# Expert layers of a mixture-of-experts kernel: the first layer's weights become the stationary operand, and the two layers swap which weights stay on chip

## The chip, the core and the metric

The kernel runs on one core of one Trainium2 chip. Its engines are named as in the profile: PE is TensorE's matmul stream and PEld its weight loads, DVE is VectorE, ACT is ScalarE, POOL is GpSimd, and SP is SyncE, which here only issues DMAs. The metric is the device time of one execution in microseconds (us). Everything is computed in float32.

## What is computed

Block-sparse attention over 4 batch entries, 8 heads, 768 tokens and a head size of 64 gives x, 3072 tokens of width 512. A router then sends each token to one of 8 experts, and each expert is two layers with a relu between them. The attention and the router are not changed; this is the part that is:

```python
N, D, E, F = (3072, 512, 8, 1024)
...
logits = x @ w_gate
expert_idx = np.argmax(logits, axis=1)
...
for e in range(E):
    lo, hi = (boundaries[e], boundaries[e + 1])
    if lo == hi:
        continue
    h = np.maximum(x_sorted[lo:hi] @ w1[e], 0.0)
    y_sorted[lo:hi] = h @ w2[e]
y = y_sorted[inv_perm]
return (gate_w[:, None] * y).astype(np.float32)
```

An expert's w1 is 512 x 1024 and its w2 is 1024 x 512, so either is 2 MB, and all eight of either are 16 MB.

## The kernel before

The kernel has three stages. The first is the attention, with the router's logits behind each pair of heads. In it x is written to a DRAM tensor `x_rows`, a token to a row of 520 numbers (512 of x, its gate weight, and room). At the very start POOL also issues the eight loads of all of w1 (`load_w1`, L94) into the resident tile `w1_all`, while SP loads the first heads' q, k and v.

The second stage (L297 to L411) sorts: from the logits DVE works out `xe`, the expert of each of 31 tiles of 128 tokens, and `g_idx` and `s_idx`, the rows that a tile gathers and scatters. The tokens of an expert start on a new tile, so at most 24 + 7 = 31 tiles are needed, and 31 are always run.

The third stage runs the 31 tiles. For tile i:

- `gather(i)` (L424, POOL, indirect DMA) brings 128 rows of x into `xg`, which has 4 buffers.
- `fetch(i)` (L430 to L432, SP) reads the tile's expert from `xe` into a register (a value load: TENSOR_LOAD and two register operations) and loads that expert's w2, 2 MB, into one of two buffers.
- `turn_x(i)` (L437) transposes the four 128 x 128 blocks of `xg` on PE into PSUM (`tpg`), and DVE copies them to `xgT` (L439).
- `layer1(i)` (L447) makes h, 128 tokens x 1024, in two PSUM banks: 8 matmuls, `xgT` as the stationary operand (the one that a weight load brings into the array) and 512 columns of `w1_all` as the moving one. A float32 matmul is two instruction pairs in the trace, each a weight load and a matmul, so this is 16 pairs. DVE does the relu of one half (L452) and ACT of the other (L453).
- `turn_h(i)` (L460) transposes h in eight blocks on PE, since the second layer needs it with its 1024 features on the partitions; DVE (L462) and ACT (L464) copy the result to `hT`.
- `layer2(i)` (L469) makes 128 tokens x 512 from 8 matmuls (16 pairs), `hT` stationary and 512 columns of the fetched w2 moving. DVE multiplies by the gate weight (`zo`, L471), and POOL scatters the rows to the output (L472).

In the source, tile i + 1's `turn_x` and `layer1` stand ahead of tile i's `turn_h` and `layer2`, and the fetch for tile i + 2 stands behind `layer2(i)`. The final order on each engine is not the source's: a scheduler of the framework orders the instructions from the dependencies and its own estimates. Each engine then runs its list in order, and a wait in a list holds up all that stands behind it there. The value loads of an engine are such list entries too.

Of the kernel before, what the change touches and what calls it, by code (L numbers as in the profile page):

```python
# [8 lines left out]
F32 = mybir.dt.float32  # L9
# [9 lines left out]
def kernel(  # L19
# [12 lines left out]
    P = 128  # L32
# [4 lines left out]
    NCH = S // P  # chunks of 128 tokens; chunk c holds the tokens NCH * p + c  # L37
    CW = NCH // 2 * P  # columns of half the chunks, within one PSUM bank
# [7 lines left out]
    NC = NT + E - 1  # tiles that the tokens take at most, each of one expert  # L46
    XW = DM + 8  # a token's row in DRAM: x, its gate weight, and room
    scale = 1.0 / float(D) ** 0.5
    # Added to a score before the scale; a masked one then lies near -1e9, whatever it was.
# [12 lines left out]
    w1_all = big.tile([P, DB, E, F], F32, name="w1_all")  # L62
# [30 lines left out]
    def load_w1(e):  # L93
        nc.gpsimd.dma_start(w1_all[:, :, e, :], moe_w1[e].rearrange("(c p) f -> p c f", p=P))  # L94
# [5 lines left out]
    def make_mask(pool):  # L100
        # Which blocks of keys (columns) a block of queries (partitions) attends to.
# [24 lines left out]
        # rows[n, t, p]: whether query NCH * p + t lies in block n.  # L126
# [38 lines left out]
    def scores(b, pr, t):  # L165
# [11 lines left out]
        for hh in range(2):  # L177
            # The scores with their sign turned, and the least of each row: minus its maximum.
# [41 lines left out]
    def route(b, pr, half, xb):  # L220
        # What the pair's columns of x add to the logits, for half of the chunks.
# [46 lines left out]
    for u in range(len(units) + LAG):  # L268
        if u < len(units):
# [7 lines left out]
            if t == 3 and n % 2 == 0 and n // 2 < E:  # L277
                load_w1(n // 2)
# [53 lines left out]
    # The first of the experts with the greatest logit.  # L332
# [9 lines left out]
    # Ranks within the expert, and how many tokens each has.  # L342
# [10 lines left out]
    # Tiles by expert, and the tiles up to and with each expert's.  # L353
# [8 lines left out]
    # The expert of each tile.  # L362
# [8 lines left out]
    # Each token's slot, from 0.  # L371
# [15 lines left out]
    # The token of each slot plus one, 0 for none.  # L387
# [31 lines left out]
    w2v = moe_w2.rearrange("e (a p) d -> p e a d", p=P)  # L419
# [9 lines left out]
    def fetch(i):  # L429
        e = nc.sync.value_load(xe[0:1, i : i + 1], min_val=0, max_val=E - 1)  # L430
# [50 lines left out]
    for i in range(2):  # L481
        gather(i)
        fetch(i)
    turn_x(0)
    layer1(0)
    for i in range(NC):
        if i + 2 < NC:
            gather(i + 2)
# [37 lines left out]
```

## Time and profile before

| | |
|---|---|
| time, median of 3 runs | 1203.21 us (1201.95 to 1203.82) |
| the profiled execution, span | 1203.9 us |
| attention, up to its last score tiles | 0 to 668.0 us |
| the sort, and the wait for the first gathers | 668.0 to 701.3 us |
| the 31 tiles, first layer-1 matmul to last layer-2 matmul | 701.3 to 1195.3 us |
| the last scatter | 1195.3 to 1203.9 us |

The profiled execution's span lies 0.7 us above the median of the timed runs. In the rows of the trace a line of a timeline is a run of equal instructions: its start, how long the run took, the engine, the source line, the operation, what it writes and reads, the shapes and the count; in brackets stands the idle time before it and what ended it. A row of PE or PEld covers latency too: the last of a run of matmuls is reported until its result is written, so the pace of a run is read from the starts, or from the run's length less the length of one. Buffers whose names differ by a number are written as one, so `w_all` is `w1_all` before and `w2_all` after, and `w` is a fetched weight tile.

### The profile page before, as it was taken

The page shows a single profiled execution, that of the slowest core. Times are in us where ns is not written, and L with a number is a line of the kernel's source. Part 1 is how long each engine was busy: PE and PEld are TensorE (multiplying, and loading weights), DVE is VectorE, ACT ScalarE, POOL GpSimd, SP SyncE. Part 2 cuts the span into 40 slices and gives each one's busy share as a digit, 9 for nine tenths or more (in the row PEclk, how much of TensorE's full clock was granted, in tenths as well). Part 3 has the DMA queues.
Part 4 walks back from the last instruction along what each step waited for, and adds up shares of the span by engine and source line. Part 5 has one row for each costly group of instructions (what it writes and reads, how often), then busy time and mean ns, then how long its engine had stood idle before and what let it go on. Part 6 is the DMA issues. An engine that isn't in the chain of part 4 may idle for free.

```text
span 1203.9 us, 15693 instructions
## 1 busy us (share of the span) xinstructions
PE 1131.7 (94%) x6132; PEld 756.1 (63%) x6132; DVE 414.1 (34%) x1032; ACT 355.5 (30%) x707; POOL 73.8 (6%) x101
## 2 busy tenths in 40 slices
PE   2899999999999999999999579999999999999996
PEld 1687878787877788788878534444444444444443
DVE  1654545554454444454444411111111111111110
ACT  0454545454545455455545000000000000000000
POOL 3000000000000000000000011111110111111100
PEclk9999999999999999999999679999999999999998
DMA  9911221112021212120000415544444555544441
GB/s 337 343 37 27 54 53 28 40 43 53 27 52 30 53 27 54 27 54 27 27 1 14 154 36 174 168 141 160 149 156 164 175 172 175 174 162 149 161 140 55
DMA packets 112269, 122.64 MB, mean 102 GB/s; under 512 B 56451, under 2 KB 72835, under 8 KB 112196
## 3 DMA queue, kind: packets, MB, share of 16 engines
q1 hardware_dynamic: 102484, 90.28, 24.9%
q0 software_dynamic: 9184, 31.33, 6.7%
q8 instruction: 50, 0.82, 0.3%
q14 instruction: 23, 0.19, 0.1%
q10 hardware_dynamic: 528, 0.02, 0.0%
HBM read 108.93 MB, written 14.52 MB: 103 GB/s over the span
## 4 chain that ended last, share of the span: by engine, by line
PE 54%; issue 38%; POOL 3%; DVE 2%; DMA 1%; SPq 0%; POOLq 0%; ACT 0%; DVEq 0%
PE op L209 21%; PE s L173 16%; PE tpe L197 12%; POOL xg L424 3%; PE lg L230 2%; PE tp L155 2%; DMA samp_i<-in_sampled_blocks_dram 1%; POOL out_dram L472 1%; PE tpx L225 1%; PE tok_ps L404 1%; DVE mask L142 0%; DVE wide L141 0%; PE bm L136 0%; SPq L84 0%; DVE oh_r L399 0%
## 5 line engine op out<-in xcount | busy, mean ns | idle before, releaser
L209 PE MATMUL op<-v_sb,eT 128*128 128x64 f32 x2304 | 278.5, 271 | 0.0
L209 PEld LDWEIGHTS op<-v_sb,eT 128*128 128x128 f32 x2304 | 272.4, 192 | 0.0
L186 ACT ACTIVATE e<-e,nmax 128x768 f32<-128x768 f32 x192 | 179.7, 936 | 243.6 <-DVE nmax L181 238.8
L447 PE MATMUL hp<-w_all,xgT 128*128 x496 | 223.2, 604 | 16.4 <-DVE xgT L439 16.4
L469 PE MATMUL zp<-w,hT 128*128 128x512 f32 x496 | 218.2, 593 | 1.1 <-DVE hT L462 1.1
L181 DVE CUSTOM_DVE_ANT_0 e<-s,mask 128x768 f32<-128x768 f32 x192 | 176.3, 954 | 103.2 <-PE s L173 103.2
L173 PE MATMUL s<-kT,qT 64*128 64x384 f32 x768 | 198.3, 525 | 7.8 <-DVE nmax L181 7.8
L447 PEld LDWEIGHTS hp<-w_all,xgT 128*128 128x128 f32 x496 | 92.7, 192 | 129.2 <-issue 105.9
L197 PEld LDWEIGHTS tpe<-ident,e 128*128 128x128 f32 x1152 | 127.5, 145 | 61.1 <-issue 26.7
L197 PE MATMUL tpe<-ident,e 128*128 128x128 f32 x1152 | 164.5, 279 | 0.0
L469 PEld LDWEIGHTS zp<-w,hT 128*128 128x128 f32 x496 | 91.8, 190 | 105.3 <-issue 103.8
L464 ACT COPY hT<-tph 128x512 f32<-128x512 f32 x31 | 18.2, 586 | 436.7 <-PE tph L460 436.7
L201 ACT COPY eT<-tpe 128x512 f32<-128x512 f32 x192 | 110.8, 577 | 51.0 <-PE tpe L197 50.5
L173 PEld LDWEIGHTS s<-kT,qT 64*128 64x128 f32 x768 | 79.2, 188 | 45.1 <-issue 19.6
L471 DVE TENSOR_SCALAR zo<-zp,xg 128x512 f32<-128x512 f32 x31 | 23.3, 750 | 204.3 <-PE zp L469 204.3
L452 DVE TENSOR_SCALAR h<-hp 128x512 f32<-128x512 f32 x31 | 21.4, 691 | 209.0 <-PE hp L447 209.0
L199 DVE COPY eT<-tpe 128x512 f32<-128x512 f32 x96 | 65.9, 687 | 15.5 <-PE tpe L197 15.3
L472 POOL DMA_INDIRECT out_dram<-zo,s_idx x31 | 31.6, 1018 | 431.3 <-DVE zo L471 431.3
L213 DVE TENSOR_SCALAR r<-ss 128x2 f32<-128x2 f32 x96 | 16.1, 167 | 88.1 <-ACT e L186 88.1
L215 DVE TENSOR_TENSOR xb<-op,r 128x128 f32<-128x128 f32 x96 | 28.0, 292 | 43.9 <-PE op L209 42.8
L308 POOL IOTA first_w_i<- 128x8 int32 x1 | 0.1, 135 | 657.4 <-PE op L209 657.4
L460 PEld LDWEIGHTS tph<-ident,h 128*128 128x128 f32 x248 | 30.0, 141 | 16.4 <-issue 16.4
(103 smaller groups left out, 484.0 us busy)
## 6 DMA issues: line engine op xcount, KB each, us to landing
w<-in_moe_w_dram SPq DMA_DIRECT2D x31, 2048.0 KB, 10.4
w_all<-in_moe_w_dram POOLq DMA_DIRECT2D x8, 2048.0 KB, 27.3
k_sb<-in_k_dram SPq DMA_DIRECT2D x32, 192.0 KB, 3.4
q_sb<-in_q_dram SPq DMA_DIRECT2D x32, 192.0 KB, 3.3
v_sb<-in_v_dram SPq DMA_DIRECT2D x16, 384.0 KB, 3.4
x_rows<-xb SPq DMA_DIRECT2D x16, 384.0 KB, 4.3
xg<-x_rows,g_idx POOLq DMA_INDIRECT x31, 7.8
out_dram<-zo,s_idx POOLq DMA_INDIRECT x31, 8.0
```

Source lines behind the costliest of these rows:

```text
L173: nc.tensor.matmul(sps[hh][:, j, :CW], lhsT=qT[r, t * P : (t + 1) * P], rhs=kT[r, j * CW : (j + 1) * CW], start=True, stop=True,)
L181: nc.vector.tensor_tensor_reduce(out=e.rearrange("p (j c) -> p j c", j=2), in0=sps[hh][:, :, :CW], in1=mask[:, t, :].rearrange("p (j c) -> ...
L186: nc.scalar.activation(e[:], e[:], AF.Exp, bias=nmax[:], scale=-1.0, accum_out=ss[:, hh : hh + 1])
L197: nc.tensor.transpose(tp[:, m, :], es[hh][:, c * P : (c + 1) * P], ident[:])
L199: nc.vector.tensor_copy(part[:], tp[:])
L201: nc.scalar.copy(part[:], tp[:])
L209: nc.tensor.matmul(op[:, hh, :], lhsT=eT[hh * NCH + c], rhs=v_sb[:, hh, c, :], start=(c == 0), stop=(c == NCH - 1),)
L424: nc.gpsimd.indirect_dma_start(out=xg[:], out_offset=None, in_=x_d[:, :], in_offset=bass.IndirectOffsetOnAxis(ap=g_idx[:, i : i + 1], axis=0),
L447: nc.tensor.matmul(hp[:, f, :], lhsT=st[i]["xT"][:, c, :], rhs=w1_all[:, c, bass.ds(e, 1), f * 512 : (f + 1) * 512].rearrange("p e f -> p ...
L460: nc.tensor.transpose(tp[:, m, :], st[i]["h"][:, (4 * g + m) * P : (4 * g + m + 1) * P], ident[:])
L469: nc.tensor.matmul(zp[:], lhsT=st[i]["hT"][:, fb, :], rhs=st[i]["w2"][:, fb, :], start=(fb == 0), stop=(fb == FB - 1))
L472: ins = nc.gpsimd.indirect_dma_start(out=out[:, :], out_offset=bass.IndirectOffsetOnAxis(ap=s_idx[:, i : i + 1], axis=0), in_=zo[:], in_of ...
```

## The change

All of w2 is now loaded at the start and stays resident (`w2_all`), and each tile's w1 is fetched instead. With w1 in a tile buffer, `layer1` takes 128 x 128 blocks of w1 as the stationary operand and the 128 tokens of `xgT` as the moving one, so that its result comes out as h with the features on the partitions. The relu writes `hT` directly; `turn_h`, the tile h and its two copies are gone. The value load on PE moves from `layer1` to `layer2`, and `fetch` moves ahead of `gather` for the first two tiles and from behind `layer2` to beside the gather for the others.

```diff
-    w1_all = big.tile([P, DB, E, F], F32, name="w1_all")
+    w2_all = big.tile([P, FB, E, DM], F32, name="w2_all")
...
-    def load_w1(e):
-        nc.gpsimd.dma_start(w1_all[:, :, e, :], moe_w1[e].rearrange("(c p) f -> p c f", p=P))
+    def load_w2(e):
+        nc.gpsimd.dma_start(w2_all[:, :, e, :], moe_w2[e].rearrange("(a p) d -> p a d", p=P))
...
         e = nc.sync.value_load(xe[0:1, i : i + 1], min_val=0, max_val=E - 1)
-        w2 = st[i]["w2"] = wp.tile([P, FB, DM], F32, name="w2")
-        nc.sync.dma_start(w2[:], w2v[:, bass.ds(e, 1)].rearrange("p e a d -> p (e a) d"))
+        w1 = st[i]["w1"] = wp.tile([P, DB, F], F32, name="w1")
+        nc.sync.dma_start(w1[:], w1v[:, bass.ds(e, 1)].rearrange("p e c f -> p (e c) f"))
...
     def layer1(i):
-        e = nc.tensor.value_load(xe[0:1, i : i + 1], min_val=0, max_val=E - 1)
-        hp = ps_h.tile([P, 2, 512], F32, name="hp")
-        h = st[i]["h"] = xp.tile([P, F], F32, name="h")
-        for f in range(2):
-            for c in range(DB):
-                nc.tensor.matmul(
-                    hp[:, f, :], lhsT=st[i]["xT"][:, c, :],
-                    rhs=w1_all[:, c, bass.ds(e, 1), f * 512 : (f + 1) * 512].rearrange("p e f -> p (e f)"),
-                    start=(c == 0), stop=(c == DB - 1),
-                )
-        nc.vector.tensor_relu(h[:, :512], hp[:, 0, :])
-        nc.scalar.activation(h[:, 512:], hp[:, 1, :], AF.Relu)
-
-    def turn_h(i):
+
         hT = st[i]["hT"] = xp.tile([P, FB, P], F32, name="hT")
         for g in range(2):
-            tp = ps_m.tile([P, 4, P], F32, name="tph", tag="m")
-            for m in range(4):
-                nc.tensor.transpose(tp[:, m, :], st[i]["h"][:, (4 * g + m) * P : (4 * g + m + 1) * P], ident[:])
+            hp = ps_h.tile([P, FB // 2, P], F32, name="hp")
+            for m in range(FB // 2):
+                fb = g * (FB // 2) + m
+                for c in range(DB):
+                    nc.tensor.matmul(
+                        hp[:, m, :], lhsT=st[i]["w1"][:, c, fb * P : (fb + 1) * P], rhs=st[i]["xT"][:, c, :],
+                        start=(c == 0), stop=(c == DB - 1),
+                    )
             if g == 0:
-                nc.vector.tensor_copy(hT[:, :4, :], tp[:])
+                nc.vector.tensor_relu(hT[:, : FB // 2, :], hp[:])
             else:
-                nc.scalar.copy(hT[:, 4:, :], tp[:])
+                nc.scalar.activation(hT[:, FB // 2 :, :], hp[:], AF.Relu)
 
     def layer2(i):
+        e = nc.tensor.value_load(xe[0:1, i : i + 1], min_val=0, max_val=E - 1)
...
     for i in range(2):
+        fetch(i)
         gather(i)
-        fetch(i)
     turn_x(0)
     layer1(0)
     for i in range(NC):
         if i + 2 < NC:
             gather(i + 2)
+            fetch(i + 2)
         if i + 1 < NC:
             turn_x(i + 1)
             layer1(i + 1)
-        turn_h(i)
         layer2(i)
-        if i + 2 < NC:
-            fetch(i + 2)
```

What the scheduler makes of it is seen in the order of instructions. First PE in the steady part of the third stage, before: one tile, from the end of one layer 2 on (the two value loads stand in the first tiles only).

```order
L469 MATMUL zp<-w2_6334,hT 128x512 x8
L437 MATMUL tpg<-ident,xg 128x128 x4
L460 MATMUL tph<-ident,h 128x128 x4
L442 TENSOR_LOAD xe
L442 ISA x2
...
L447 ISA
L447 MATMUL hp<-w_all,xgT 128x512
...
L460 MATMUL tph<-ident,h 128x128 x4
```

The same place after.

```order
L438 MATMUL tpg<-ident,xg 128x128 x4
L463 ISA
L463 MATMUL zp<-w_all,hT 128x512
L463 ISA
L463 MATMUL zp<-w_all,hT 128x512
L450 MATMUL hp<-xgT,w_6631 128x128 x32
L463 ISA
L463 MATMUL zp<-w_all,hT 128x512
```

Between the transposes of x and the first layer that reads them there stood four transposes of h; now two of the eight layer-2 matmuls of the tile before stand there, and the other six follow the first layer.

Second, PE at the start of the third stage, before: behind the last of 17 value loads two tiles' transposes and then the first layer.

```order
L442 TENSOR_LOAD xe
L442 ISA x2
L437 MATMUL tpg<-ident,xg 128x128 x8
L447 ISA
L447 MATMUL hp<-w_all,xgT 128x512
```

And after.

```order
L438 MATMUL tpg<-ident,xg 128x128 x16
L460 TENSOR_LOAD xe
L460 ISA x2
L460 TENSOR_LOAD xe
L460 ISA x2
...
L450 MATMUL hp<-xgT,w_6319 128x128 x32
```

Four tiles' transposes, and behind them five of the value loads, have moved ahead of the first tile's first layer.

Third, SP at the same place, before: the first fetch stands behind one value load.

```order
L255 DMA x_rows<-gw 768x1x8
L430 TENSOR_LOAD xe
L430 ISA x2
L432 ISA
L432 DMA w_6321<-in_moe_w2_dram 128x8x512
L430 TENSOR_LOAD xe
```

And after, the last of the value loads ahead of the first fetch, and the two fetches.

```order
L431 TENSOR_LOAD xe
L431 ISA x2
L433 ISA
L433 DMA w_6319<-in_moe_w_dram 128x4x1024
L433 ISA
L433 DMA w_6332<-in_moe_w_dram 128x4x1024
```

Seventeen value loads now stand ahead of the first fetch.

## Rows read from the trace of the kernel before

**Rows 1.** The page: span, then each engine's busy time, share and instructions.

```profile
span 1203.9 us, 15693 instructions
PE 1131.7 (94%) x6132; PEld 756.1 (63%) x6132; DVE 414.1 (34%) x1032; ACT 355.5 (30%) x707; POOL 73.8 (6%) x101
```

**Rows 2.** Sums by stretch: length, busy time per engine (instructions), granted clock, DMA share, GB/s.

```profile
0.00:60.00 60.00, 33.07 (x193) 24.59 (x194) 23.51 (x61) 15.96 (x31) 9.56 (x23) 1.00 0.99 340
701.30:1195.30 494.00, 476.47 (x1357) 226.99 (x1356) 80.45 (x122) 33.71 (x62) 56.94 (x57) 1.00 0.45 151
```

**Rows 3.** Timeline of PE over one tile of the third stage.

```profile
909.27 0.60 PE L460 MATMUL tph<-ident,h 128*128 128x128 f32 x4
909.70 7.03 PE L469 MATMUL zp<-w,hT 128*128 128x512 f32 x16
916.57 0.60 PE L437 MATMUL tpg<-ident,xg 128*128 128x128 f32 x4
917.01 0.60 PE L460 MATMUL tph<-ident,h 128*128 128x128 f32 x4
918.18 7.13 PE L447 MATMUL hp<-w_all,xgT 128*128 x16 [0.57 <-DVE xgT L439]
925.15 0.60 PE L460 MATMUL tph<-ident,h 128*128 128x128 f32 x4
```

**Rows 4.** Timeline of DVE around the end of the tile before.

```profile
900.89 0.75 DVE L471 TENSOR_SCALAR zo<-zp,xg 128x512 f32<-128x512 f32 x1 [6.54 <-PE zp L469]
901.56 0.68 DVE L439 COPY xgT<-tpg 128x512 f32<-128x512 f32 x1
```

**Rows 5.** Timeline of the weight loads near the attention's end.

```profile
664.24 0.74 PEld L230 LDWEIGHTS lg<-wg,xT 128*128 128x128 f32 x6 [0.38 <-ACT xT L227]
664.90 2.76 PEld L209 LDWEIGHTS op<-v_sb,eT 128*128 128x128 f32 x24
```

**Rows 6.** Page, groups of weight loads: busy, mean ns of one | idle before.

```profile
L209 PEld LDWEIGHTS op<-v_sb,eT 128*128 128x128 f32 x2304 | 272.4, 192 | 0.0
L469 PEld LDWEIGHTS zp<-w,hT 128*128 128x128 f32 x496 | 91.8, 190 | 105.3 <-issue 103.8
```

**Rows 7.** Timelines of PEld and PE where transposes give way to `op`.

```profile
661.33 0.64 PEld L209 LDWEIGHTS op<-v_sb,eT 128*128 128x128 f32 x5
...
660.99 0.61 PE L197 MATMUL tpe<-ident,e 128*128 128x128 f32 x4
661.44 0.56 PE L209 MATMUL op<-v_sb,eT 128*128 128x64 f32 x4
```

**Rows 8.** Waits from 700 us on: in total, how often, the longest.

```profile
PE hp L447 <- DVE xgT L439: 16.4, 29, 0.6
```

**Rows 9.** Lines L432 (all, then the second fetch) and L424: issue to landing.

```profile
DMA to landing us min/median/max: 8.2/10.4/12.8
...
DMA to landing us min/median/max: 12.8/12.8/12.8
...
DMA to landing us min/median/max: 3.5/7.8/9.3
```

**Rows 10.** Value loads on SP and PE: ns min/median/max, first and last start.

```profile
L430 SPq TENSOR_LOAD <-xe x29: 263/263/278, 680.0 to 696.1; - x29
...
L442 PEldq TENSOR_LOAD <-xe x8: 299/300/306, 689.3 to 694.1; - x8
```

**Rows 11.** Timeline at the start of the third stage: POOL's fourth gather, then PE.

```profile
698.98 0.95 POOL L424 DMA_INDIRECT xg<-x_rows,g_idx  x1 [0.30 <-issue]
...
698.69 1.08 PE L437 MATMUL tpg<-ident,xg 128*128 128x128 f32 x4 [5.38 <-DMA xg<-x_rows,g_idx]
```

**Rows 12.** Timeline of weight loads at the lower clock (1.2 GHz), in the sort.

```profile
682.86 10.31 PEld L404 LDWEIGHTS tok_ps<-oh_c,oh_r 128*128 128x128 f32 x48 [8.61 <-DVE oh_r L399]
```

**Rows 13.** Page: the DMA queue that POOL feeds; then DVE's first wait for data.

```profile
q0 software_dynamic: 9184, 31.33, 6.7%
...
19.36 0.16 DVE L117 CAST samp<-samp_i 24x3 f32<-24x3 int32 x1 [17.56 <-DMA samp_i<-in_sampled_blocks_dram]
```

More of the change, by code (lines that the diff above doesn't have):

```diff
@@ L277 @@
             if t == 3 and n % 2 == 0 and n // 2 < E:
-                load_w1(n // 2)
+                load_w2(n // 2)
             if t == 4 and n + 1 < len(pairs):
@@ L418 @@
     ps_z = ctx.enter_context(tc.tile_pool(name="ps_z", bufs=2, space=PSUM))
-    w2v = moe_w2.rearrange("e (a p) d -> p e a d", p=P)
+    w1v = moe_w1.rearrange("e (c p) f -> p e c f", p=P)
     st = [{} for _ in range(NC)]
@@ L441, in layer1 @@
     def layer1(i):
-        e = nc.tensor.value_load(xe[0:1, i : i + 1], min_val=0, max_val=E - 1)
-        hp = ps_h.tile([P, 2, 512], F32, name="hp")
-        h = st[i]["h"] = xp.tile([P, F], F32, name="h")
-        for f in range(2):
-            for c in range(DB):
-                nc.tensor.matmul(
-                    hp[:, f, :], lhsT=st[i]["xT"][:, c, :],
-                    rhs=w1_all[:, c, bass.ds(e, 1), f * 512 : (f + 1) * 512].rearrange("p e f -> p (e f)"),
-                    start=(c == 0), stop=(c == DB - 1),
-                )
-        nc.vector.tensor_relu(h[:, :512], hp[:, 0, :])
-        nc.scalar.activation(h[:, 512:], hp[:, 1, :], AF.Relu)
-    def turn_h(i):
         hT = st[i]["hT"] = xp.tile([P, FB, P], F32, name="hT")
         for g in range(2):
-            tp = ps_m.tile([P, 4, P], F32, name="tph", tag="m")
-            for m in range(4):
-                nc.tensor.transpose(tp[:, m, :], st[i]["h"][:, (4 * g + m) * P : (4 * g + m + 1) * P], ident[:])
+            hp = ps_h.tile([P, FB // 2, P], F32, name="hp")
[6 more added lines that the diff above has]
+                    )
             if g == 0:
-                nc.vector.tensor_copy(hT[:, :4, :], tp[:])
+                nc.vector.tensor_relu(hT[:, : FB // 2, :], hp[:])
             else:
-                nc.scalar.copy(hT[:, 4:, :], tp[:])
+                nc.scalar.activation(hT[:, FB // 2 :, :], hp[:], AF.Relu)
     def layer2(i):
+        e = nc.tensor.value_load(xe[0:1, i : i + 1], min_val=0, max_val=E - 1)
         zp = ps_z.tile([P, DM], F32, name="zp")
         for fb in range(FB):
-            nc.tensor.matmul(zp[:], lhsT=st[i]["hT"][:, fb, :], rhs=st[i]["w2"][:, fb, :], start=(fb == 0), stop=(fb == FB - 1))
+            nc.tensor.matmul(
+                zp[:], lhsT=st[i]["hT"][:, fb, :], rhs=w2_all[:, fb, bass.ds(e, 1), :].rearrange("p e d -> p (e d)"),
+                start=(fb == 0), stop=(fb == FB - 1),
+            )
         zo = xp.tile([P, DM], F32, name="zo")
```

## The prediction

> **What bounds the kernel now.** I read the page's first line, then the sums by stretch, then the timeline of one tile. PE is busy for 94% of the 1203.9 us span [rows 1], and in the 494.0 us of the third stage it is busy for 476.5, at the full clock, with the DMA engines at 0.45 [rows 2]. So a tile costs what PE's list costs. By the starts in [rows 3], from one `zp` to the point a tile later: layer 2 takes 916.57 - 909.70 = 6.87 us for 16 pairs (0.429 each), the transposes of x 0.44, half of the transposes of h and the wait behind them 918.18 - 917.01 = 1.17, of which 0.57 is PE waiting for `xgT`, layer 1 925.15 - 918.18 = 6.97, and the other half of the transposes of h 0.43 (as 909.70 - 909.27). The sum is 15.88 us a tile, and 31 tiles are 492.3 of the stage's 494.0. What is left over is the slow clock of the first matmuls, less the first tile's transposes.
>
> **Layer 1, the term that decides.** It had 16 pairs with 512 columns. It gets 32 matmuls, 64 pairs, each with a new 128 x 128 weight load and only 128 moving columns. The columns are as many as before (64 x 128 = 16 x 512), but the loads are four times as many. A pair is either bound by its columns, 0.429 / 4 = 0.107 us (the eight transposes of 128 columns run at 0.44 / 4 = 0.11, [rows 3]), or by its load. The load's price is seen where few columns hide it: 24 loads for `op`, with 64 columns, take 2.76 us, so (2.76 - 0.19) / 23 = 0.112 each, and with 8 columns for `lg` (0.74 - 0.19) / 5 = 0.110 [rows 5], where 0.19 is one load [rows 6]. So a load runs while the matmul before it streams, and columns cost nothing below the load's own time. A load is no slower beside a stream either: 190 ns behind 512 columns, 192 behind 64 [rows 6]. What no row has is a long run in which load and columns are equally long. The nearest is a boundary: the first load for `op` starts at 661.33, beside the last of four 128-column transposes, and its matmul starts 0.11 later [rows 7]. The bounds for a pair are therefore 0.110 and the 0.112 plus whatever a near tie costs; I take 0.112 and let the range reach to 0.120. Layer 1 is then 64 x 0.112 = 7.17 us, 0.20 more than the 6.97 now.
>
> **Transposes of h and the wait.** Eight transposes and the 0.57 us wait go: 0.43 + 1.17 = 1.60 us a tile off PE. The wait is 16.4 us over 29 tiles [rows 8]. It came from the copy to `xgT`, which had four transposes of h (0.43) to hide behind. Now two layer-2 matmuls, four pairs, 4 x 0.429 = 1.72 us, stand there. The copy is late on DVE, because `zo` (0.75) of the tile before goes first: `zo` starts at 900.89, the copy at 901.56, and it ends at 902.24 [rows 4]. The transposes of x began about 0.2 before `zo`, and layer 1 is due 0.44 + 1.72 = 2.16 after they begin, at about 902.85. So 0.6 us of cover is left, and the wait goes. Next in line is `hT`: its relus (a DVE and an ACT operation, as before) end under the 12 pairs, 5.1 us, of layer 2 that follow layer 1. DVE and ACT each lose a copy; neither is near a bound, so this is worth nothing.
>
> **Per tile.** 6.87 + 0.44 + 7.17 = 14.48 us against 15.88, and 31 x 1.40 = 43.4 us off.
>
> **The fetch.** A fetch of w1 starts when layer 1 of the tile two before has freed its buffer, and is needed 2 x 14.48 - 7.17 = 21.8 us later. A 2 MB fetch lands in 8.2 to 12.8 us beside gathers and scatters [rows 9]; for w1 the rows in DRAM are twice as long, so I keep this. It is hidden, with 9 us to spare. For the third tile, whose layer 1 follows only one layer 1 and one layer 2, the cover is 14.0 us, still enough. Gathers have four buffers and some 28 us of cover against at most 9.3.
>
> **The start of the stage.** Here the change costs time. On SP, 17 value loads now stand ahead of the first fetch. They are (696.1 - 680.0) / 28 = 0.575 us apart [rows 10], so the first fetch is issued near 687.5 instead of 678.3 and the second near 688. The second of the two took 12.8 us [rows 9], so both have landed by 701. That is in time for the first layer 1, but now they run beside the first gathers, which start at about 695. On PE, layer 1 used to follow two tiles' transposes (the first at 698.69) and began at 701.30 [rows 2, 11]. Now it stands behind four tiles' transposes and then five value loads, 5 x (694.1 - 689.3) / 7 = 3.4 us [rows 10], which cannot start before the fourth gather has landed, as PE's list waits for it. That gather is issued at 698.98 [rows 11]. Landing takes 3.5 us alone and up to 9.3 beside fetches [rows 9], so it lands between 702.5 and 708.3. The fetch stops disturbing it at 701, so I take 704.4. Layer 1 then starts at 704.4 + 0.2 + 3.4 = 708.0, 6.7 us later than now; the bounds are 5 and 10.6. The clock is low there (a load takes 10.31 / 48 = 0.215, [rows 12], twice 0.107) and stays low for some first microseconds in both kernels, which I count as equal.
>
> **The start of the kernel.** Loading w2 instead of w1 brings the same 16 MB in rows of 2 KB, not 4 KB. The first 60 us run with the DMA engines 0.99 busy [rows 2], and DVE's first wait for data lasts until 19.36 [rows 13], because SP's small loads share the engines with POOL's large ones. If POOL's packets became half as long, SP's loads would pass sooner: half of the 16.5 us since the weight loads began at about 2.8 is the upper bound, say 6 to 8 us gained. But POOL's queue moved 4096 rows of w1, 31 x 128 gathered and 3072 scattered rows, 11136 in all, in 9184 packets [rows 13], so short rows share a packet there. Two rows of w2 are as long as one of w1. I take zero, and 8 us as the bound of the gain.
>
> **The sum.** From the profiled 1203.9: - 43.4 + 6.7 = 1167.2. The end does not move (the last scatter follows the last `zo` as before). The profile lies 0.7 above the median, so 1166.5; I predict 1166.
>
> **Rivals.** First, and this ends slower: weight loads that do not hide beside 128 columns. A pair would cost load plus columns, 0.112 + 0.109 = 0.221, layer 1 14.14 us, a tile 21.45, and the kernel 1203.2 + 31 x 5.57 + 6.7 = 1383. It is decided by the pair alone: the tie with now is at (15.88 - 6.87 - 0.44 - 6.7 / 31) / 64 = 0.131 us. For it: no long run at this balance exists, and the margin from 0.112 to 0.131 is small. Against it: [rows 5 to 7], where full loads run beside streams without a trace of delay. I give it 5%. The Trainium skill speaks for it: "TensorE: Matmul & The Clock Gate", in Part 3, The mechanism, says that a weight load overlaps a running matmul only where the row groups differ, and here all pairs use all 128 rows; by that rule the kernel would take the 1383. The same page, under Back-to-back issue gap, has 81 ns a pair sustained at 128 columns against 56 for a lone matmul; an estimate by that ratio, 0.112 x 1.45 = 0.162 a pair, gives 31 x 1.8 + 6.7 more than now, 1266. [rows 5] speak against both: 0.112 with a 64-column stream inside it leaves no room for a sum.
>
> Second: a small wait comes back on every tile, by `xgT` late behind `zo`, or by a pair of 0.120 to 0.125. That is 0.5 to 0.8 us a tile, 16 to 25 us, and gives about 1182 to 1191. 12%.
>
> Third: the short rows of w2 let the start pass sooner: 1158 to 1161. 14%.
>
> Fourth, slower as well: the fetch is late. With two buffers a tile cannot be shorter than half of the fetch's landing time and layer 1 together; it decides from 21.8 us on, and at 26 us the tile would be 16.6, the kernel 1203 + 31 x 0.7 + 6.7 = 1232. The longest landing is 12.8. 1%.
>
> **How the numbers follow.** My forecast has 67%, 1160 to 1176; with the rivals' 5, 12, 14 and 1%, and 1% for no change. 0.2% of the time, 2.4 us, is what a measurement of this kernel tells from no change. Faster takes the forecast, the second and the third rival: 0.93; same 0.01; slower 0.06. The range takes in the early start and layer-1 pairs up to 0.120 (31 x 64 x 0.008 = 16 us): 1155 to 1184.
>
> **What would show it.** In the new profile: layer 1's loads 0.112 apart in the steady part, and one tile 14.5 us from `tpg` to `tpg` (above 0.131 apart, I am wrong in sign). No wait of PE for `xgT` or `hT`, and none for a landing of w1 after the second tile. The first layer-1 matmul near 708, behind five value loads. Fetch landings below 13 us. DVE's first wait for data ending near 19.4 (nearer 12 shows the third rival).

## The result, and the profile after

The changed kernel takes 1166.11 us (median; 1164.76 to 1168.5) against 1202.58 for the kernel before beside it: a ratio of 0.9696, with a 95% interval of 0.9679 to 0.9712. It is 3.0% faster, and the forecast was 1166.

The engines' line of the page of the changed kernel (span 1166.8 us), and then the sums of the third stage (length, busy time of PE, PEld, DVE, ACT and POOL with instructions, granted clock, DMA share, GB/s); they answer to [rows 1, 2]:

```profile
PE 1108.9 (95%) x7372; PEld 858.2 (74%) x7372; DVE 395.9 (34%) x1001; ACT 340.5 (29%) x676; POOL 75.0 (6%) x101
```

```profile
711.00:1162.00 451.00, 449.94 (x2588) 327.41 (x2588) 61.49 (x90) 18.51 (x31) 57.00 (x57) 1.00 0.46 166
```

PE is still what bounds the stage (449.9 of 451.0 us busy), but its list is 43 us shorter. Now PE over one tile, from its transposes of x to the next tile's, and DVE beside the next tile's (they answer to [rows 3, 4]):

```profile
906.58 0.60 PE L438 MATMUL tpg<-ident,xg 128*128 128x128 f32 x4
907.01 1.88 PE L463 MATMUL zp<-w_all,hT 128*128 x4
908.73 7.31 PE L450 MATMUL hp<-xgT,w 128*128 128x128 f32 x64
915.88 5.32 PE L463 MATMUL zp<-w_all,hT 128*128 x12
921.03 0.60 PE L438 MATMUL tpg<-ident,xg 128*128 128x128 f32 x4
...
923.18 7.31 PE L450 MATMUL hp<-xgT,w 128*128 128x128 f32 x64
```

```profile
921.23 0.75 DVE L468 TENSOR_SCALAR zo<-zp,xg 128x512 f32<-128x512 f32 x1 [7.98 <-PE zp L463]
921.90 0.68 DVE L440 COPY xgT<-tpg 128x512 f32<-128x512 f32 x1
```

Layer 1 is 64 pairs in 915.88 - 908.73 = 7.15 us, 0.1117 a pair, where 0.112 was forecast. The tile is 921.03 - 906.58 = 14.45 us, where 14.48 was forecast (before: 15.88). No row of PE has an idle time, so the wait of [rows 8] is gone here: the copy to `xgT` ends at 922.58, and layer 1 begins at 923.18.

The last six tiles are different. PE and, in the last line, DVE, near the end:

```profile
1140.28 0.60 PE L438 MATMUL tpg<-ident,xg 128*128 128x128 f32 x4
1140.72 1.02 PE L463 MATMUL zp<-w_all,hT 128*128 x2
1141.89 7.41 PE L450 MATMUL hp<-xgT,w 128*128 128x128 f32 x64
```

```profile
1141.15 0.68 DVE L440 COPY xgT<-tpg 128x512 f32<-128x512 f32 x1
```

Here the order has two layer-2 pairs (one matmul) between the transposes and layer 1, not four, since a value load on PE took a place. Layer 1 could begin 0.44 + 0.86 = 1.30 after the transposes, but the copy ends at 1141.83, and it begins 1.61 after. Its first weight load waits as well and starts only with its matmul, which makes layer 1 0.1 longer. These tiles take 14.86 us, 0.41 more than the others: 2.5 us in all.

The start of the stage: SP's line of the fetch (an operation, how often, ns min/median/max, first and last start), its first two fetches, then PE up to the first layer 1, whose line (x128) holds the first two tiles' (they answer to [rows 10, 11]):

```profile
L433 SPq EVENT_SEMAPHORE  x35: 17/17/6522, 687.6 to 1105.2; - x35
```

```profile
694.56 0.98 SPq L433 DMA_DIRECT2D w<-in_moe_w_dram  x2
```

```profile
701.84 1.09 PE L438 MATMUL tpg<-ident,xg 128*128 128x128 f32 x4 [8.30 <-DMA xg<-x_rows,g_idx]
...
707.14 1.09 PE L438 MATMUL tpg<-ident,xg 128*128 128x128 f32 x4 [0.94 <-DMA xg<-x_rows,g_idx]
711.05 16.27 PE L450 MATMUL hp<-xgT,w 128*128 128x128 f32 x128 [2.82 <-issue]
```

SP's 17 value loads ended at 687.5, as forecast, but the first fetch was issued at 694.56: for 6.52 us SP waited at a semaphore, and the profile puts the end of that wait down to `s_idx`, the sort's last instruction. The fetches then ran beside the first gathers, the fourth tile's transposes came at 707.14 (forecast 704.4), and five value loads on PE followed. The first layer 1 begins at 711.05, 3.05 later than forecast.

Last, what surrounds the stage: issue to landing in us; POOL's closing DRAIN, after and then before the change; and DVE's first wait for data (it ended at 19.36 in [rows 13]).

```profile
w<-in_moe_w_dram SPq DMA_DIRECT2D x31, 2048.0 KB, 7.7
...
xg<-x_rows,g_idx POOLq DMA_INDIRECT x31, 3.5
out_dram<-zo,s_idx POOLq DMA_INDIRECT x31, 2.1
```

```profile
L516 POOLq DRAIN  x3: 51/104/2953, 1163.0 to 1166.5; - x3
```

```profile
L521 POOLq DRAIN  x3: 51/104/7010, 1196.1 to 1203.7; - x3
```

```profile
L117 DVE CAST samp<-samp_i x1: 157/157/157, 18.5 to 18.5; 24x3 f32<-24x3 int32 x1
```

The fetches and the gathers land sooner than in [rows 9], and the scatters in 2.1 us and not in 8.0. From the start of the last layer-2 matmul to the end it is 5.2 us, and was 9.25: POOL's DRAIN after the last scatter takes 2.95 us and not 7.01.

Between the two profiled executions the 37.1 us (1203.9 - 1166.8) lie so: the sort ends at 694.1 (`s_idx` starts) and ended at 693.9, +0.2; from there to the first layer 1 it is 16.9 us and was 7.4, +9.5; from there to the last layer-2 matmul 450.5 and was 493.4, -42.9; and the tail, -4.0.

### The profile page after: what moved, and what is told of

It is laid out like the page before. It is cut to its first block, busy times and chain, and to the rows that moved or that the text cites. A ratio compares the mean times of both kernels' runs of the same rounds, so it can differ in the third digit from the quotient of the medians.

```text
span 1166.8 us, 17998 instructions
## 1 busy us (share of the span) xinstructions
PE 1108.9 (95%) x7372; PEld 858.2 (74%) x7372; DVE 395.9 (34%) x1001; ACT 340.5 (29%) x676; POOL 75.0 (6%) x101
## 4 chain that ended last, share of the span: by engine, by line
PE 56%; issue 37%; POOL 4%; DVE 2%; DMA 1%; SPq 0%; POOLq 0%; ACT 0%; DVEq 0%
PE op L209 21%; PE s L173 16%; PE tpe L197 12%; POOL xg L424 3%; PE lg L230 2%; PE tp L155 2%; DMA samp_i<-in_sampled_blocks_dram 1%; POOL out_dram L469 1%; PE tpx L225 1%; PE tok_ps L404 1%; DVE mask L142 0%; DVE wide L141 0%; PE bm L136 0%; SPq L84 0%; DVE oh_r L399 0%
## 5 line engine op out<-in xcount | busy, mean ns | idle before, releaser
L450 PEld LDWEIGHTS hp<-xgT,w 128*128 128x128 f32 x1984 | 227.3, 193 | 20.5 <-DVE xgT L440 11.6
L450 PE MATMUL hp<-xgT,w 128*128 128x128 f32 x1984 | 228.9, 277 | 3.8 <-issue 2.8
L463 PE MATMUL zp<-w_all,hT 128*128 x496 | 222.3, 592 | 0.0
L463 PEld LDWEIGHTS zp<-w_all,hT 128*128 128x128 f32 x496 | 89.8, 190 | 91.3 <-issue 91.3
L457 ACT ACTIVATE hT<-hp 128x512 f32<-128x512 f32 x31 | 18.5, 597 | 460.3 <-PE hp L450 460.3
L173 PEld LDWEIGHTS s<-kT,qT 64*128 64x128 f32 x768 | 79.4, 189 | 45.3 <-issue 19.4
L455 DVE TENSOR_SCALAR hT<-hp 128x512 f32<-128x512 f32 x31 | 21.5, 692 | 136.9 <-issue 117.0
L230 PEld LDWEIGHTS lg<-wg,xT 128*128 128x128 f32 x192 | 23.8, 190 | 17.5 <-ACT xT L227 17.5
```

The lines of the kernel that those rows point to most:

```text
L173: nc.tensor.matmul(sps[hh][:, j, :CW], lhsT=qT[r, t * P : (t + 1) * P], rhs=kT[r, j * CW : (j + 1) * CW], start=True, stop=True,)
L230: nc.tensor.matmul(lg[:, m, :], lhsT=xT[:, m, :], rhs=wg[:, pr, :], start=True, stop=True)
L450: nc.tensor.matmul(hp[:, m, :], lhsT=st[i]["w1"][:, c, fb * P : (fb + 1) * P], rhs=st[i]["xT"][:, c, :], start=(c == 0), stop=(c == DB - 1),)
L463: nc.tensor.matmul(zp[:], lhsT=st[i]["hT"][:, fb, :], rhs=w2_all[:, fb, bass.ds(e, 1), :].rearrange("p e d -> p (e d)"), start=(fb == 0), ...
```

## Experiments

The theory: layer 1 costs the longer of a load and a stream, and at 128 x 128 the two are almost equal; the stage's start is late because w1's buffers share memory with the sort; the two other terms (the tail, the kernel's start) come with the resident weights. The rivals are in each expectation. Each ratio is to the kernel before, run beside it.

| run | us | ratio, 95% interval |
|---|---|---|
| the change | 1166.1 | 0.9696 (0.9679 to 0.9712) |
| e1_gap | 1157.2 | 0.9622 (0.9590 to 0.9653) |
| e2_halfcols | 1171.1 | one run |
| e3_halfload | 1176.8 | one run |
| e3b_halfboth | 1077.9 | one run |
| e6_resid | 1197.0 | 0.9945 (0.9924 to 0.9966) |
| e5_both | 1150.5 | 0.9563 (0.9534 to 0.9592) |
| e7_early_x | 1152.2 | 0.9596 (0.9550 to 0.9642) |
| e8_defer | 1141.1 | 0.9485 (0.9455 to 0.9514) |
| e4_onebuf | 1190.4 | one run |
| e9_rows2k | 1158.8 | one run |
| e10_before_again | 1204.0 | one run |
| e11_w1_2k | 1192.5 | one run, 1204.6 beside it |

### What a pair costs

**Half of the columns.**

```diff
-                        hp[:, m, :], lhsT=st[i]["w1"][:, c, fb * P : (fb + 1) * P], rhs=st[i]["xT"][:, c, :],
+                        hp[:, m, : P // 2], lhsT=st[i]["w1"][:, c, fb * P : (fb + 1) * P], rhs=st[i]["xT"][:, c, : P // 2],
...
```

> Layer 1 moves only 64 of each tile's 128 tokens, so each matmul has 64 moving columns behind the same 128 x 128 load; the relus copy these 64 columns twice, and half of the tokens are left out. The changed kernel had 0.1117 us a pair. Theory, the load bounds the pair: still 0.112, layer 1 7.15 us, the tile 14.45, the kernel about 1166. Rival, the columns bound it and the load is hidden with room: 0.055 to 0.06 a pair, layer 1 3.5 to 3.9 us, the tile 10.9 to 11.2, the kernel about 1060. Rival, load and columns overlap only in part: in between, in proportion to the columns that were in the sum.

PE's timeline of one steady layer 1 and of the first one, and a stretch inside the first one:

```profile
911.30 7.25 PE L451 MATMUL hp<-xgT,w 128*128 128x64 f32 x64
918.39 5.37 PE L464 MATMUL zp<-w_all,hT 128*128 x12
```

```profile
707.86 13.88 PE L451 MATMUL hp<-xgT,w 128*128 128x64 f32 x64 [2.84 <-issue]
```

```profile
712.00:716.00 4.00, 4.00 (x21) 4.00 (x20) 0.69 (x1) 0.00 (x0) 0.00 (x0) 0.50 0.00 0
```

Steady: (918.39 - 911.30) / 64 = 0.1108 a pair. Half of the moving columns were taken away and next to nothing was gained, so the load bounds the pair. That the kernel as a whole takes 5 us more than the change has another reason, told in the last section: the whole first layer 1 ran at the lower clock (0.50 granted) and took 13.7 us.

**Half of the load.**

```diff
-                        hp[:, m, :], lhsT=st[i]["w1"][:, c, fb * P : (fb + 1) * P], rhs=st[i]["xT"][:, c, :],
+                        hp[: P // 2, m, :], lhsT=st[i]["w1"][:, c, fb * P : fb * P + P // 2], rhs=st[i]["xT"][:, c, :],
...
-                zp[:], lhsT=st[i]["hT"][:, fb, :], rhs=w2_all[:, fb, bass.ds(e, 1), :].rearrange("p e d -> p (e d)"),
+                zp[:], lhsT=st[i]["hT"][: P // 2, fb, :], rhs=w2_all[: P // 2, fb, bass.ds(e, 1), :].rearrange("p e d -> p (e d)"),
```

> Layer 1 loads only the first 64 columns of each 128 x 128 block of w1 (half of the hidden units is left out, and layer 2 sums over the 64 rows that are left); 128 columns still move. Theory, a load is bound by the columns of the stationary tile and the pair by the longer of load and stream: the load falls to 0.056, the stream of 128 columns bounds the pair at 0.107, layer 1 is 6.85 us, the tile 14.15 and the kernel 1166 - 31 x 0.3 = 1157. Rival, a load costs by its 128 rows: the pair stays at 0.112 and the time at 1166. Rival, load and stream add in part: the pair falls below 0.107.

PE's timeline of a tile:

```profile
911.51 7.20 PE L450 MATMUL hp<-xgT,w 128*64 128x128 f32 x64
918.64 5.41 PE L463 MATMUL zp<-w_all,hT 64*128 x12
923.99 0.66 PE L438 MATMUL tpg<-ident,xg 128*128 128x128 f32 x4
...
926.48 7.20 PE L450 MATMUL hp<-xgT,w 128*64 128x128 f32 x64
```

Inside layer 1 the pairs start 0.109 to 0.110 apart: below 0.1117, and the same as the transposes' 0.44 / 4. So with a short load the stream bounds the pair, at 0.109 and not at the 0.107 that a quarter of a 512-column matmul gave. The time went the other way than the theory had it (the tile 14.97, the kernel 1176.8), by a part of the edit itself: layer 2 now used 64 rows of the array, layer 1 and the transposes 128, and at each of the four changes a tile PE lost 0.14 to 0.20 us (918.64 to 923.99 is 5.35 for 12 pairs that take 5.15 without a change of rows). That is 0.67 a tile, against the 0.16 that the pairs gained. Where PE goes from 64 rows to 128, the weight load isn't ahead of its matmul: the first transpose's starts at 923.98, beside the matmul's 923.99, where in the change it starts 0.43 ahead (906.15 and 906.58).

**Both halves.** The two edits at once.

> Both halves at once: 64 stationary and 64 moving columns in layer 1 (three quarters of its work are left out, and half of layer 2's sum). Theory, the longer of load and stream: 0.056 a pair, layer 1 3.6 us, the tile 10.9, the kernel 1166 - 31 x 3.55 = about 1056. Rival, issuing an instruction pair costs 0.11 whatever its size (the 8-column matmuls of the router are also 0.110 apart): the pair stays at 0.110 to 0.112 and the kernel at 1166. Rival, a load is bound by its rows alone: 0.112 as well, but then the run with half the load shows 0.112 too, not 0.107.

```profile
914.78 3.94 PE L451 MATMUL hp<-xgT,w 128*64 128x64 f32 x64
918.65 0.69 PE L464 MATMUL zp<-w_all,hT 64*128 x1
```

3.87 / 64 = 0.0605 a pair. So 0.11 is no cost of issuing an instruction. (The tile is 11.72 and not 10.9: layer 1, with one of the four changes of rows in its 3.87, takes 0.27 more than the 3.6 expected, and the other three changes take 0.53.) The three runs together show, for pairs of this size, the rule on which the forecast rested: a pair costs the longer of load (0.111 for 128 columns of weights) and stream (0.109 for 128 moving columns), with no sum in it. That a load goes by its columns is what the Trainium skill states ("TensorE: Matmul & The Clock Gate", LDWEIGHTS); the trace agrees, 0.111 for 128 columns and no more than 0.0605 for 64.

### The start of the stage

**Memory for w1 apart from the sort's.**

```diff
     xp = ctx.enter_context(tc.tile_pool(name="xp", bufs=2))
+    gap = ctx.enter_context(tc.tile_pool(name="gap", bufs=1))
+    gap.tile([P, 2 * F], F32, name="gap")
     wp = ctx.enter_context(tc.tile_pool(name="wp", bufs=2))
```

> One edit: 8 KB of each partition are left unused ahead of the two w1 buffers, so that these no longer lie on memory of the sort (the dropped tile h had kept them apart before the change). Theory, memory reuse: in the changed kernel SP held the first fetch until 694.56 because its buffer lay on memory that the sort still read, and the scheduler, which knew it, set 17 value loads of SP ahead of that fetch and two more tiles' transposes and five value loads of PE ahead of the first layer 1. With the memory apart the first fetch is issued near 678.3, as before the change, the first layer-1 matmul starts at 701.3 to 702 instead of 711.05, and the kernel takes 1166.1 - 9.5 = 1156 to 1157. Rival A, the new order of the start itself (the fetches beside the gathers) is what costs: the first layer 1 stays at 706 or later, and the time above 1161. Rival B, the start is earlier but the tiles behind it give it back (a longer slow clock, late fetches): 1161 to 1166. Both theories leave the tile at 14.45 us, and at 14.86 for the last ones.

SP's first fetches, and PE at the first layer 1:

```profile
674.87 1.65 SPq L435 DMA_DIRECT2D w<-in_moe_w_dram  x2
```

```profile
697.25 15.31 PE L452 MATMUL hp<-xgT,w 128*128 128x128 f32 x128
```

The sort ended at 690.4 in this execution, so the first layer 1 stands 6.9 us behind it; it was 16.9 in the change and 7.4 before. The 10 us go with one thing, 8 KB of memory a partition. Of them 2.5 are given back: the value loads that left the start went to the tiles, and now twelve of these take 14.86 us and not six. The median is 8.9 us below the change's, and the intervals of the two ratios do not touch.

### The cover of the copy

**x transposed a tile earlier**, in the kernel with the gap.

```diff
...
         if i + 2 < NC:
-            gather(i + 2)
             fetch(i + 2)
+        if i + 3 < NC:
+            gather(i + 3)
+        if i + 2 < NC:
+            turn_x(i + 2)
         if i + 1 < NC:
-            turn_x(i + 1)
             layer1(i + 1)
         layer2(i)
```

> The kernel with the gap of 8 KB, and the transposes of x set one tile earlier (a tile's x is transposed before the layer 1 of the tile ahead of it, with a fifth buffer for the gathered rows). Theory, the cover of the copy to xgT: in the kernel with the gap, 12 of the tiles last 14.86 us instead of 14.45, because only one layer-2 matmul and a value load stand between the transposes and layer 1; with a whole layer 1 and layer 2 between, all tiles take 14.45, and the kernel 12 x 0.41 = 4.9 us less than with the gap alone, 1152. Rival, the 14.86 come from the value load on PE itself and not from the copy: those tiles stay at 14.86 and the kernel at 1157.

```profile
920.62 0.60 PE L440 MATMUL tpg<-ident,xg 128*128 128x128 f32 x4
921.06 7.31 PE L452 MATMUL hp<-xgT,w 128*128 128x128 f32 x64
928.21 7.03 PE L465 MATMUL zp<-w_all,hT 128*128 x16
```

Every tile but the first and the last takes 14.45 us, also those with a value load on PE, and the kernel's median is 5.0 us below the one with the gap alone. The intervals of the two ratios overlap (one of the four executions here took 1160.7), so it is the tiles, and not the medians, that show it: the 14.86 came from the copy's cover, not from the value load. The order of a tile is now transposes, layer 1, layer 2, with nothing between that has to hide anything.

### The parts of the change apart

**The residence swap alone.**

```diff
-        hT = st[i]["hT"] = xp.tile([P, FB, P], F32, name="hT")
-        for g in range(2):
...
+        for f in range(2):
+            for c in range(DB):
+                nc.tensor.matmul(
+                    hp[:, f, :], lhsT=st[i]["xT"][:, c, :], rhs=st[i]["w1"][:, c, f * 512 : (f + 1) * 512],
...
+        turn_h(i)
         layer2(i)
```

> The residence swap alone: w2 resident, w1 fetched per tile, but layer 1 as before the change (x stationary, 512 columns of w1 moving) and h transposed. Theory, all of the gain is in the swap of layer 1: the tile stays at 15.88 us, PE waits for xgT as before, and the kernel takes 1203, give or take the start (its tile h keeps w1's buffers off the sort's memory, so the first fetch is early: within 1200 to 1207). Rival, fetching w1 instead of w2 is itself worth something or costs something (the fetch no longer meets the scatter and the gather; its landing falls from 10.4 to 7.7): then 1190 or less, or above 1210. On the tail, which was 4.0 us shorter in the changed kernel: if it is short here as well (last zo to the end 4.6 us, not 8.6), it goes with the weights fetched; if long, with the order of the last tile's work.

PE's wait in a tile, and POOL's closing DRAIN:

```profile
913.68 7.13 PE L447 MATMUL hp<-w,xgT 128*128 128x512 f32 x16 [0.57 <-DVE xgT L440]
```

```profile
L523 POOLq DRAIN  x3: 51/104/2945, 1191.6 to 1195.2; - x3
```

The tile is 15.88 us as before, with the same wait of 0.57. So the tile's gain is layer 1's alone. But the swap of residence is not nothing: 6.8 us, of which the short tail is 4.0.

**The swap of layer 1 alone.** With w1 resident it was not tried; this run has neither matrix resident.

```diff
-    w2_all = big.tile([P, FB, E, DM], F32, name="w2_all")
...
+        w2 = st[i]["w2"] = wp.tile([P, FB, DM], F32, name="w2")
+        nc.sync.dma_start(w2[:], w2v[:, bass.ds(e, 1)].rearrange("p e a d -> p (e a) d"))
...
-                zp[:], lhsT=st[i]["hT"][:, fb, :], rhs=w2_all[:, fb, bass.ds(e, 1), :].rearrange("p e d -> p (e d)"),
+                zp[:], lhsT=st[i]["hT"][:, fb, :], rhs=st[i]["w2"][:, fb, :],
```

> The swap of layer 1 without the swap of residence: nothing is resident, both w1 and w2 of a tile are fetched (4 MB a tile, two buffers each; 48 KB of each partition are left unused ahead of them, so that they don't lie on the sort's memory). Theory, the fetches hide: the tile stays at 14.45 us; the 16 MB of the start and the value loads on PE go, so the start is 8 to 12 us earlier and no tile takes 14.86: about 1140 to 1145. Rival, bandwidth: the start of the kernel shows 333 GB/s at a share of 1.01; 4.19 MB of weights and 0.53 MB of rows are 4.72 MB a tile, 14.2 us at that rate, so any loss of a few per cent beside gathers and scatters makes the DMA engines the bound: the tile 15 to 17 us, the kernel 1160 to 1225. The latency formula of the prediction's fourth rival (half of the landing and layer 1) would not show this, since it decides only from a landing of 21.8 us.

The sums of a long stretch, the landing of the fetches, and the DRAIN:

```profile
720.00:1130.00 410.00, 407.60 (x2353) 294.93 (x2352) 57.12 (x84) 16.72 (x28) 53.80 (x54) 1.00 0.88 318
```

```profile
w<-in_moe_w_dram SPq DMA_DIRECT2D x62, 2048.0 KB, 11.9
```

```profile
L514 POOLq DRAIN  x3: 40/107/6352, 1141.9 to 1148.8; - x3
```

Neither theory nor rival, but between them: with the DMA engines 0.88 busy, the steady tiles take 14.45 to 15.1 us. The start of the kernel gained more than expected (the sort ends at 676.9), the tail was long, and the first layer 1 came 9.8 us behind the sort. So PE's list of 14.45 us is close to what the DMA engines need for 4 MB and a tile's rows.

### The fetch

**One buffer for w1.**

```diff
-    wp = ctx.enter_context(tc.tile_pool(name="wp", bufs=2))
+    wp = ctx.enter_context(tc.tile_pool(name="wp", bufs=1))
```

> The changed kernel with one buffer for w1 instead of two, so that a tile's fetch can only start when the layer 1 of the tile before is done. Theory, the prediction's model of the fetch (a tile cannot be shorter than layer 1 and what the fetch takes from the end of one layer 1 to its landing; with two buffers half of the sum): 7.15 + 0.19 to the issue + 7.7 to the landing = 15.0 us a tile where PE's list wants 14.45, and PE waits 0.5 to 0.7 for w1 in every tile; the kernel about 1166 + 30 x 0.6 = 1184. Rival, a fetch that meets no gather lands faster than 7.1: then the tile stays at 14.45 and the second buffer was worth nothing, 1166. Rival, the waiting tiles put the fetch back beside gathers and scatters (10.4 as in the kernel before): the tile 17.7, 1265.

Two tiles' layer 1, an ordinary one and a bad one:

```profile
886.68 7.38 PE L450 MATMUL hp<-xgT,w 128*128 128x128 f32 x64 [0.52 <-DMA w<-in_moe_w_dram]
...
1058.16 9.01 PE L450 MATMUL hp<-xgT,w 128*128 128x128 f32 x64 [1.98 <-DMA w<-in_moe_w_dram]
```

In most tiles PE waits 0.3 to 1.0 us for w1 and the tile is 15.0 to 15.7: the model's 15.0. In five it waits 1.7 to 2.2 (a fetch lands in 7.4 to 9.1 us, 7.7 in the median), and in two of the five, after waits of 1.98 and 2.19, the granted clock then fell to 0.50 and layer 1 took 1.63 us more. That makes the 1190.4 rather than 1184. The second buffer is worth some 24 us, and with it nothing of the fetch is seen.

**Rows of 2 KB, in two issues.**

```diff
-        nc.sync.dma_start(w1[:], w1v[:, bass.ds(e, 1)].rearrange("p e c f -> p (e c) f"))
+        for h in range(2):
+            f = slice(h * 512, (h + 1) * 512)
+            nc.sync.dma_start(w1[:, :, f], w1v[:, bass.ds(e, 1), :, f].rearrange("p e c f -> p (e c) f"))
```

> The changed kernel with w1 fetched in two halves of its columns, so in rows of 2 KB as w2 was fetched before the change, and two issues for 4 KB rows' one. Two questions. Landing: a fetch landed in 10.4 us (median) before the change and lands in 7.7 now. If the length of the rows decides, the second half lands 10 us or more after the first issue; if it was the scatter and the gather issued within 2.4 us of the fetch before the change, it lands within 8.5. Tail: from the start of the last zo to the end it is 8.6 us where w2 is fetched per tile and 4.6 where it is resident (POOL's closing DRAIN 7.0 or 6.4 us against 2.95). If that goes with the number or the length of the fetched rows, it is long here; if with w2 itself or its place in the order, it stays at 4.6. The time: 1166 (short) or 1170 (long); the tile 14.45 in both.

```profile
w<-in_moe_w_dram SPq DMA_DIRECT2D x62, 1024.0 KB, 5.1
```

```profile
699.70 15.05 PE L452 MATMUL hp<-xgT,w 128*128 128x128 f32 x128
```

```profile
L518 POOLq DRAIN  x3: 51/104/2962, 1153.3 to 1156.8; - x3
```

Short rows do not make a fetch slow. That leaves its neighbours for the 10.4 us of [rows 9]: before the change, a tile's fetch, scatter and gather were issued at 916.76, 917.80 and 919.13, and the last fetch, which has a scatter but no gather behind it, landed in the 8.2 that is the minimum there; in the change the fetch goes out at 916.07, and the other two at 922.26 and 923.59. The tail stays short, so it does not go with the rows fetched per tile. The 7 us that this run has below the change were not expected. In its profile the sort ends 5.4 us earlier, and the first layer 1 comes only 11.0 us behind it, not 16.9: here the scheduler set nine transposes and no value load ahead of it, though the fetch was still held until 689.1 (the sort ended at 688.7). Read so, of the 10 us at the start some 4 are the late fetch, and some 6 the two more tiles' transposes and the value loads that the scheduler set ahead because of it; no run took these two apart.

### The start of the kernel and the tail

**Loads of w2 held back**, in the kernel with the early transposes.

```diff
-    def load_w2(e):
+    def load_w2(e, ss):
+        nc.gpsimd.tensor_copy(w2_all[0:1, 0, e, 0:2], ss[0:1, :])
         nc.gpsimd.dma_start(w2_all[:, :, e, :], moe_w2[e].rearrange("(a p) d -> p a d", p=P))
...
-                load_w2(n // 2)
+                load_w2(n // 2, scored[u][1])
```

> The kernel before this one (gap, x transposed a tile earlier), with each of the eight 2 MB loads of w2 held back until the attention of its pair of heads has begun (a copy of two values into the tile, which waits for that pair's sums, stands ahead of the load on POOL). Theory, the price that the prediction put on its third rival: SP's small loads no longer share the DMA engines with 16 MB, DVE's first wait for data ends near 8 us or earlier instead of 18.5, PE begins some 10 us earlier, and the kernel takes 8 to 12 us less than the one before it, 1140 to 1144. Rival, the attention's own chain sets the start and the loads were only beside it: less than 2 us. Rival, the loads now disturb the loads of the later heads: part of the gain is lost again, 1145 to 1150.

DVE's first wait for data, and the loads of w2 (first and last start):

```profile
L118 DVE CAST samp<-samp_i x1: 157/157/157, 8.4 to 8.4; 24x3 f32<-24x3 int32 x1
```

```profile
L95 POOL DMA_DIRECT2D w_all<-in_moe_w_dram x8: 882/882/1089, 37.7 to 591.5; - x8
```

The wait ends at 8.4, the sort 9.8 us earlier than in the kernel ahead of it (679.1 and 688.9), and the median falls by 11.2 us. That is the price of the large loads beside the small ones, in full, and so more than the third rival, with shorter rows, could have given. This is the fastest kernel of the study: 5.2% below the kernel before, 2.1% below the change.

**The kernel before, again.**

> The kernel before, unchanged, for a second profile of it. Two readings rest on one profile of it so far. First, the tail: POOL's closing DRAIN took 7.0 us, against 2.95 in eight profiles where w2 is resident (6.4 with both fetched). If that belongs to the kernel, it is 6 to 7 us again, and last zo to the end 8 to 9 us; if it was that execution, about 3. Second, the start: DVE's wait for the table of sampled blocks ended at 19.4 us, against 14.4 to 18.5 in the nine profiles with w2 resident. If the third rival (2-KB rows of the resident weights let small loads pass) has a part in the gain, it ends at 18 to 20 again; if the start only varies from run to run, it may as well end at 15.

```profile
L521 POOLq DRAIN  x3: 51/104/7012, 1194.4 to 1202.0; - x3
```

DVE's first wait ends at 18.5 this time (19.4 in [rows 13]), and the sort at 692.0.

**The resident w1 loaded in rows of 2 KB**, in the kernel before.

```diff
-        nc.gpsimd.dma_start(w1_all[:, :, e, :], moe_w1[e].rearrange("(c p) f -> p c f", p=P))
+        for h in range(2):
+            f = slice(h * 512, (h + 1) * 512)
+            nc.gpsimd.dma_start(w1_all[:, :, e, f], moe_w1[e, :, f].rearrange("(c p) f -> p c f", p=P))
```

> The kernel before, with each of the eight loads of the resident w1 cut in two halves of its columns, so in rows of 2 KB as w2's are (16 issues on POOL for 8). It isolates the third rival. If the length of the rows sets how soon SP's small loads pass, DVE's wait for the table of sampled blocks ends some 3 to 4 us earlier than in the kernel before on the same chip, near 15, and the kernel takes 1199 to 1201; if not, it ends within 1 us of that kernel's and the time is 1203 to 1204. The tail is as in the kernel before.

```profile
L523 POOLq DRAIN  x3: 51/104/2944, 1187.0 to 1190.5; - x3
```

```profile
L119 DVE CAST samp<-samp_i x1: 156/156/156, 13.9 to 13.9; 24x3 f32<-24x3 int32 x1
```

```profile
L96 POOL DMA_DIRECT2D w_all<-in_moe_w_dram x16: 748/748/4361, 2.8 to 32.9; - x16
```

The 7 us of DRAIN belong to the kernel before (7.01 twice), and they went with an edit that touches only how POOL loads the resident weights: w2 is still fetched per tile here. So the tail goes with what POOL's own queue has been given: 2.94 to 2.96 us wherever that was 16 MB in rows of 2 KB, 7.01 with rows of 4 KB, 6.35 with none. The last scatter itself isn't it: it lands 2.1 us after its issue in the kernel before, in the change, in e5_both, e6_resid and e11_w1_2k alike. Why a DRAIN a millisecond later should know of the loads stays open. The expectation that the tail is as before was wrong, and it makes a third of the 12 us that this run gained; most of the rest is the start. There the run doesn't isolate the rows' length, because POOL, with 16 issues, had to wait for landings itself, and its loads are spread until 32.9 us and not 10.7.

## Why the prediction was right, point by point

- **A pair.** Forecast 0.112, measured 0.1117, and the three runs with halves show the mechanism: the longer of load and stream. The first rival, load plus stream, is out. So is the rule of the Trainium skill ("TensorE: Matmul & The Clock Gate", Part 3, The mechanism) that a weight load overlaps a running matmul only where the row groups differ; here all pairs use all rows, the trace does not agree, and by that rule the pair would have taken 0.22. The same section also names the background weight buffer as a case in which a load is pulled ahead; no run here shows which buffer a load went to. Nor is the ratio of 81 to 56 ns (the Trainium skill, same page, Back-to-back issue gap) seen here: a pair takes 0.1117, and its stream alone 0.109.
- **The tile.** Forecast 14.48, measured 14.45 for most, so the transposes of h and the wait are worth what they were said to be worth. e6_resid shows that none of it is the residence.
- **The cover of the copy.** 0.6 us was to be left; by the rows it is 923.18 - 922.58 = 0.60, of which some 0.06 is needed between copy and matmul. What the step missed is that in the last six tiles only one of its "two layer-2 matmuls" stands there. There the first form of the second rival, `xgT` late behind `zo`, came true, for 2.5 us.
- **The fetch.** No wait of PE for w1, landings of 7.5 to 8.7 where 8.2 to 12.8 was kept; the model of the fourth rival gives 15.0 for one buffer, and most tiles took 15.0 to 15.4. What it left out is the DMA engines' rate: with 4 MB a tile they are 0.88 busy and tiles stretch, at landings far below 21.8.
- **The start of the stage.** This term was mis-sized: +6.7 forecast, +9.5 measured against the sort's end, within the bounds of 5 and 10.6. The step that failed is the issue of the first fetch "near 687.5": its 17 value loads ended there, but the fetch waited for the sort to leave the memory of its buffer. That the value loads and the extra transposes stood ahead at all had the same cause, which the prediction took from the order without asking for it. e1_gap shows it.
- **The start of the kernel.** Zero was taken, and the profiled execution has nothing: the first wait ends at 18.5 against 19.4, the sort at 694.1 against 693.9. But in the eight other profiles with w2 resident at the start the wait ends between 14.4 and 17.7, and the sort between 687.9 and 692.4; the kernel before has 18.5 and 19.4, 692.0 and 693.9. So a few microseconds of the third rival's gain seem to have come in most executions, and the change's profiled one was the longest of its four. Whether the rows' length does it was not isolated.
- **The end.** "The end does not move" was wrong by 4.0 us, from POOL's DRAIN, which no step had looked at.

So the sum was right partly by chance: -43.4 + 6.7 was forecast between the profiles, and -42.9 + 9.5 + 0.2 - 4.0 came, 36.7 and 37.1. The large term is right by its mechanism; the two small ones that were off, +2.8 and -4.0, cancelled.

## What to carry to other kernels

Where loads and streams are of one length, cost a pair by the longer of the two: exchanging which operand stands still is then free, and whatever transposes it removes is the gain. When a tile leaves a pool, ask what slides onto memory that others still use: 8 KB of each partition fewer here held a fetch for 7 us changed, through the scheduler, the orders of SP and PE. Bulk loads that are needed half a millisecond later should not be given to the DMA engines ahead of the small ones that the first instruction waits for.

## What the runs showed of the hardware that was not expected

- A first layer 1 with 64 moving columns behind full loads kept the granted clock at 0.50 (1.2 GHz) for all of its 13.7 us, though PE was busy without a break (e2_halfcols, 712 to 716: 4.00 of 4.00 us busy). In the change, with 128 columns, the clock rose within the first layer 1 (0.50 at 713, 1.00 from 715 on), and with 64 columns behind half loads as well (e3b_halfboth, 1.00 from 714 on, layer 1 begun at 709.87). In the steady part of e2_halfcols the same pairs take 7.1 at 2.4 GHz.
- After a wait of 1.98 us in the middle of the stage the clock fell to 0.50, and the next layer 1 took 9.01 us and not 7.38 (e4_onebuf): a late fetch was paid almost twice. After a wait of 2.04 us in the same run (layer 1 at 950.34) the clock stayed at 1.00.
- Going from matmuls on 128 rows to matmuls on 64 and back cost 0.67 us a tile in four changes (e3_halfload).
- 2 MB asked for as two transfers of 1 MB, in rows of half the length, landed in 5.1 us each, issued 0.57 us apart, so 5.7 in all, where one transfer took 7.7 (e9_rows2k; medians).
- POOL's closing DRAIN took 2.9 us where POOL had loaded 16 MB in rows of 2 KB earlier in the kernel, 7.0 with rows of 4 KB (two profiles), and 6.4 with no such loads (e5_both).
